# Lightning attention with balanced MoE on one core: two-input rank arithmetic, digits on VectorE, an earlier compaction operand, and ten weight loads queued ahead of the first gathers

## The chip, the cores and the metric

The kernel runs on one core of a Trainium2 chip. The metric is the device time of one execution in microseconds (us). Each kernel of a comparison ran on the same chip as the kernel before, in alternating rounds. A run is called slow if it is over 1.5% above the fastest run of the same kernel. Two terms of the profile: the DMA share is the mean busy share of the core's 16 DMA engines (the sum of the packets' times, which can come out over 1: 1.15 from 131 to 155 us in the kernel before), and the granted clock is TensorE's clock as a share of full speed (0.895 on average there).

## The reference

Four sequences of 768 tokens, 8 heads of 64, go through a decaying linear attention. The result, 3072 tokens of 512, is routed to 8 experts with a capacity of 384 each, in the order of the largest logit anywhere, and each token goes through its expert's two matrices.

```python
def _moe_ref(x, w_gate, w1, w2):            # x: 3072 x 512, w1: 8 x 512 x 1024, w2: 8 x 1024 x 512
    logits = x @ w_gate
    flat = logits.flatten()
    order = np.argsort(-flat)
    # ... greedy: a token takes the expert of its pair if it has none and the expert has room (cap = N // E)
    for e in range(E):
        mask = assigned == e
        h = np.maximum(x[mask] @ w1[e], 0.0)
        out[mask] = h @ w2[e]
```

## The kernel before

It has three stages. **Attention** works through 24 tiles of 128 tokens with a hand-made order of instructions; each tile's q, k and v are loaded on SyncE's queue, and its result xs is stored to DRAM there. **Routing** ranks the logits by counting, and gives the token numbers (`perm`) of each expert. The **experts** gather their tokens with indirect DMAs, run two matmuls, and scatter the result. All weight loads (sixteen of 1 MB), gathers and scatters are issued by GpSimd, in program order. In this kernel's trace no recorded landing of that queue comes before that of an earlier issue: the load issued at 180.40 landed at 198.28, the scatter issued at 181.53 at 198.92, and the one issued at 183.82, behind one more load, at 204.59.

```python
# attention: 256 bytes of each token and head go to each place in SBUF
def _load(self, g, name, src):
    b, t = divmod(g, 6)
    a = self.io.tile([128, 8, 64], F32, tag=name, name=name)
    self.nc.sync.dma_start(out=a, in_=src[b, :, t * 128 : (t + 1) * 128, :].rearrange("h p d -> p h d"))
# ...
d["xs"] = self.wk.tile([128, 4, 2, 64], F32, tag="xs", name="xs", bufs=3)   # stored to x_dram

# ranks of a group of tiles: one-input operations on VectorE
y = rc.tile([P, n], F32, name=f"y{a}")
V.tensor_scalar(y, vc, self.lo[:, 0:1], self.sc[:, 0:1], OP.add, OP.mult)
V.tensor_scalar(y, y, 1.0, self.VB - 1.0, OP.max, OP.min)
# ...

# the experts' order of issue; later holds the weight loads that are left
later = list(later)                          # range(8, 16)
for _ in range(2):                           # right after the gathers of experts 0 and 1
    moe.load_w(later.pop(0))
# ... two more when the next token numbers come
def experts():
    for n in range(16):
        # ...
        yield from moe.up(jobs[n], n % 8)
        # ... transposes of the next expert, gathers of the expert after the next three
        if later:
            moe.load_w(later.pop(0))
        for c in range(len(jobs[n]["perms"])):
            yield from moe.down(jobs[n], n % 8, c)      # matmuls, copy to oe (4 buffers), scatter
            if later and c == 0:
                moe.load_w(later.pop(0))
```

Of the kernel before, what the change touches and what calls it, by code (L numbers as in the profile page):

```python
# [23 lines left out]
class _Router:  # L24
# [11 lines left out]
    def constants(self):  # L36
# [36 lines left out]
        V.memset(self.ind2[:, 64:128, :], 0.0)  # L73
        self.i_kt = iota("i_kt", [P, P, 24], [[1, P], [0, 24]], 1)
# [17 lines left out]
        self.gbase = iota("gbase", [1, 9, 24], [[384, 9], [0, 24]], 1, 0, F32)  # L92
# [54 lines left out]
    def ranks(self, L, a, b):  # L147
# [7 lines left out]
        V.tensor_scalar(y, vc, self.lo[:, 0:1], self.sc[:, 0:1], OP.add, OP.mult)  # L155
        V.tensor_scalar(y, y, 1.0, self.VB - 1.0, OP.max, OP.min)
        V.tensor_scalar(zc, y, MAGIC, MAGIC, OP.add, OP.subtract)
# [8 lines left out]
        V.tensor_scalar(y, zc, 1.0 / 4096.0, -0.5 + 1.0 / 8192.0, OP.mult, OP.add)  # L166
        V.tensor_scalar(q1, y, MAGIC, MAGIC, OP.add, OP.subtract)
# [18 lines left out]
    def extras(self, L, a, b):  # L186

        nc, rc, P = self.nc, self.rc, 128
        V, G = nc.vector, nc.gpsimd
        n = b - a  # L190
        Z = rc.tile([P, n, 8], F32, name=f"Z{a}")
        H = rc.tile([P, n, 8], F32, name=f"H{a}")
        G.tensor_scalar(Z, L[:, a:b, :], self.lo[:, 1:2], self.sc[:, 1:2], OP.add, OP.mult)
        G.tensor_scalar(Z, Z, 1.0, self.ZB - 1.0, OP.max, OP.min)
        G.tensor_scalar(Z, Z, MAGIC, MAGIC, OP.add, OP.subtract)
        G.tensor_scalar(H, Z, 1.0 / 1024.0, -0.5 + 1.0 / 2048.0, OP.mult, OP.add)
        G.tensor_scalar(H, H, MAGIC, MAGIC, OP.add, OP.subtract)
        G.tensor_copy(self.zp[:, a:b, :, 0], H)
        G.tensor_scalar(H, H, -1024.0, None, OP.mult)
        G.tensor_tensor(self.zp[:, a:b, :, 1], Z, H, OP.add)  # L200

    def warm(self, us):

        for _ in range(int(us / 0.11) if self.spare is not None else 0):
            self.nc.tensor.matmul(self.spare, self.identb,
                                  self.i_kt.rearrange("p k t -> p (k t)")[:, 0:256],
                                  start=True, stop=True)
# [12 lines left out]
    def first(self, L, sp):  # L220
# [32 lines left out]
        for t in range(22, 24):  # L253
# [7 lines left out]
        _, nm2 = settle(count(z2, lambda: self.more(1)), self.ones[64])  # L261
        z3 = sp.tile([P, 24], BF16, name="z3")
        V.tensor_scalar(z3, zB, nm2, 100.0, OP.subtract, OP.min)
        nps, nm3 = settle(count(z3), self.ones[1])
        self.extras(L, 0, 24)
# [6 lines left out]
        V.tensor_tensor(Gm, self.i_g8, g8[:, None, :].to_broadcast([P, 9, 24]), OP.is_equal)  # L272
        cum = sp.tile([P, 9, 24], BF16, name="cum")
# [3 lines left out]
        pos = ps.tile([P, 9, 24], F32, tag="pos")  # L277
        posf = pos.rearrange("p g t -> p (g t)")
        nc.tensor.matmul(posf, self.ones3[0:1, :], self.gbase.rearrange("p g t -> p (g t)"),
                         start=True, stop=False)  # L280
        nc.tensor.matmul(posf, self.sltm, Gm.rearrange("p g t -> p (g t)"), start=False,
                         stop=False)
        nc.tensor.matmul(posf, self.ones[1], cum.rearrange("p g t -> p (g t)"), start=False,
                         stop=True)
        cps9 = ps.tile([P, 9], F32, tag="cnt")
        nc.tensor.matmul(cps9, self.ones[1], cum[:, :, 23], start=True, stop=True)
        sl = sp.tile([P, 9, 24], F32, name="sl")
        V.tensor_tensor(sl, pos, Gm, OP.mult)
        slot = sp.tile([P, 24], F32, name="slot")
        V.reduce_sum(slot, sl.rearrange("p g t -> p t g"), axis=AX.X)  # L290
# [18 lines left out]
        self.warm(3.0)  # L309
        for t in range(24):  # L310
            nc.tensor.matmul(pe1, A[:, :, t], B1v[:, :, :, t], start=(t == 0), stop=(t == 23))
        perm0 = st.tile([P, 6], I32, name="perm0")
        with nc.allow_low_precision(reason="token numbers are exact"):
            V.reduce_sum(perm0, pe1.rearrange("p a j -> p j a"), axis=AX.X)
        yield perm0.rearrange("p (e j) -> p e j", j=3)

# [6 lines left out]
                        zpv[:, :, None, :].to_broadcast([P, 24, 5, 16]), OP.mult)  # L323
        V.tensor_tensor(R5[:, :, :, 16], B5, self.i_t[:, 0:5, :].rearrange("p j t -> p t j"),
# [3 lines left out]
        self.warm(1.2)  # L328
# [61 lines left out]
    def steps(self, rest):  # L390
# [24 lines left out]
        for i in range(1, 7):  # L415
# [6 lines left out]
            for r in range(3):  # L422
                ind = sp.tile([P, 5, P], BF16, tag="indc")
                for c in range(5):
                    V.tensor_scalar(ind[:, c, :], self.kvec[r], zr[:, c : c + 1], None, OP.is_le)  # L425
# [74 lines left out]
        for c in range(5):  # L500
            V.tensor_scalar(A5[:, c, :], self.kvec[2], slot[:, c : c + 1], None, OP.is_equal)
# [251 lines left out]
def _exact_path(ctx, tc, L, router, moe, dram):  # L753
# [150 lines left out]
    nc.tensor.matmul(ppf, router.ones3[0:1, :], router.gbase[:, 0:8].rearrange("p g t -> p (g t)"),  # L904
# [19 lines left out]
class _Attn:  # L924
# [11 lines left out]
    LATE = dict(kph=(82.8, 86.36, 90.63, 92.36, 102.76, 107.19, 110.24), kpl=(84, 87.49,  # L936
                93.13, 94.38, 105.5, 109.86, 113.46), vs=(86.47, 89.87, 92.11, 99.11,
                100.13, 107.97, 116.19, 117.82), vh=(87.64, 94.24, 95.44, 100.66, 101.71,
                111.46, 118.28, 118.97), vl=(88.74, 96.24, 97.98, 101.76, 103.5, 112.33,
                119.71, 122.06), Tq=(82.96, 86.42, 92.65, 96.65, 100.91, 105.29, 108.01,  # L940
                113.13), qh=(84.83, 87.13, 93.73, 97.36, 102.25, 106, 109.73, 113.84),
                ql=(85.66, 88.14, 95.79, 98.86, 104.12, 107.25, 111.66, 114.86), Tk=(85.37,
                87.02, 89.58, 95.81, 102.12, 107.15, 112.29, 115.02), kT=(86.26, 88.74,
                91.35, 97.65, 103.44, 108.53, 113.6, 119.27), S=(87.48, 91.55, 97.86,
                102.58, 106.43, 110.74, 115.48, 120.03), h0=(83.51, 88.45, 94.78, 99.49,
                103.55, 108.56, 113.17, 116.45, 121), h1=(84.17, 89.11, 93.07, 98.83,
                104.21, 107.9, 112, 117.11, 122.17), l0=(84.34, 89.34, 96.39, 101.57,
                104.72, 109.79, 114.2, 117.35, 125.19), l1=(85, 90.61, 93.92, 100.31,
                105.38, 109.13, 112.94, 118.01, 125.93), m0=(85.25, 90.89, 97.37, 102.89,
                107.36, 111.72, 117.21, 120.84, 126.01), m1=(85.86, 91.5, 95.63, 101.15,  # L950
                106.75, 111.11, 115.58, 121.45, 126.75), I=(88.2, 92.27, 96.27, 100.53,
                104.28, 108.93, 112.75, 117.51, 122.23, 126.09), X=(88.83, 93.11, 97.11,
                101.37, 104.54, 109.99, 113.59, 118.14, 123.05, 127.49), ST=(84.69, 90.41,
                0, 99.85, 105.75, 109.31, 114.34, 121.21, 0), sth=(85.85, 91.34, 0, 101.2,
                106.68, 110.95, 115.27, 122.83, 0), stl=(83.7, 87.54, 92.72, 0, 102.23,
                107.85, 112.34, 116.67, 123.98, 0), xs=(90, 94.58, 98.25, 102.83, 106.64,
                111.05, 116.06, 119.87, 124.58, 129.11), Tx=(84.23, 91.09, 95.35, 99.02,
                103.67, 108.47, 111.83, 116.83, 120.75, 125.35, 129.88), xh=(85.34, 91.85,
                96.06, 100.15, 104.87, 109.22, 112.66, 117.77, 121.66, 126.29, 130.82),
                xl=(86.86, 93.32, 97.05, 100.97, 106.04, 110.45, 115.46, 118.67, 123.38,  # L960
                128.51, 131.5), G=(83.86, 90.04, 94.11, 99.48, 103.3, 107.61, 111.46,
                116.22, 119.43, 124.43, 129.27, 132.26), lg=(87.46, 91.27, 95.71, 100.23,
                104.04, 108.45, 112.26, 117.27, 120.48, 125.85, 130.08, 133.07))
# [290 lines left out]
def kernel(  # L1254
# [22 lines left out]
    moe = _Moe(ctx, tc, identb, x_dram, moe_w1, moe_w2, out, 8)  # L1277
    with ExitStack() as actx:
        attn = _Attn(actx, tc, q, k, v, lam, moe_w_gate, identf, logits, x_dram)
        const_steps = router.constants()  # L1280
        steps, end = router.constants(), attn.END
        others = [(t, lambda: next(steps, None))
                  for t in (-3.0, -1.0, 3.5, end + 123.19, end + 129.5)]
        others += [(end + t, lambda i=i, h=h: router.ranges(logits, 14, h and attn.spare(h), i))
                   for i, (t, h) in enumerate(((91.95, 0), (94.48, 15), (95.19, 0),
                                               (98.58, 16), (99.46, 0)))]
        others += [(end + t, lambda a=a, b=b: router.ranks(logits, a, b))
                   for t, a, b in ((120.57, 0, 16), (126.60, 16, 22))]
        others += [(end + t, lambda m=m: moe.load_w(m)) for m, t in
                   enumerate((104.63, 108.99, 114.71, 118.84, 126.0, 126.1, 126.2, 126.3))]  # L1290
        with tc.manual_schedule():
            attn.run(others)
    moe.open(ctx)
    fi = _route_and_moe(ctx, tc, logits, router, moe, range(8, 16))
    _check_and_mend(ctx, tc, logits, router, moe, dram, fi)


# [28 lines left out]
```

## Time and profile before

| | us |
|---|---|
| median of 4 runs (range) | 292.0 (291.58 to 293.32) |
| profiled span | 290.0 |
| last logits | 140.39 |
| first token numbers (perm) | 156.95 |
| first transposes of gathered tokens | 164.55 |
| oe copies held by scatters | 16.6, in three waits |

The prediction below shows the stretches, waits and timelines of this kernel. The first lines are from the timeline of SyncE's queue, with start, length, queue and operation in the columns:

```profile
97.93 0.37 SPq L1017 DMA_DIRECT2D qf<-in_q_dram  x1
99.62 0.34 SPq L1193 DMA_DIRECT2D x_dram<-xs  x1
100.70 0.37 SPq L1017 DMA_DIRECT2D vf<-in_v_dram  x1
```

GpSimd's first weight load of this kernel, in its timeline, with start, length, queue and operation in the columns:

```profile
106.25 1.01 POOL L576 DMA_DIRECT2D w<-in_moe_w_dram  x1
```

### The profile page before, as it was taken

How to read it: one execution, taken by the hardware profiler on the slowest of the kernel's cores; microseconds unless marked ns; L12 is line 12 of the kernel's file. 1: busy time of each engine (PE TensorE's matmuls, PEld its weight loads, DVE VectorE, ACT ScalarE, POOL GpSimd, SP SyncE). 2: the span in 40 equal slices, each digit the busy share in tenths (PEclk: the TensorE clock that was granted, in tenths of full speed). 3: DMA queues.
4: the chain of work that ended last, by engine and by line, in shares of the span. 5: the costliest groups of instructions: out<-in, count | busy, mean ns of one | idle time of the engine just before them, and what ended most of it. 6: DMA issues, size and time to landing. Idle time of an engine off the chain costs nothing.

```text
span 290.0 us, 8784 instructions
## 1 busy us (share of the span) xinstructions
PE 231.8 (80%) x3552; PEld 184.0 (63%) x3552; DVE 185.2 (64%) x570; ACT 154.9 (53%) x273; POOL 188.5 (65%) x212
## 2 busy tenths in 40 slices
PE   1779999999999899845562799990698999899970
PEld 0669888988888688734442676660455776577740
DVE  5688989898989999998658768780276750000000
ACT  6588888888897678520000144520325654576640
POOL 8999999999999889955522866542533155454220
PEclk9999999999999999995555579996589999999995
DMA  6999999989899839999993699999995236334121
GB/s 148 253 229 245 251 268 244 250 217 239 218 221 217 221 82 199 229 232 227 222 209 64 72 182 204 209 209 238 231 240 159 75 91 128 94 95 84 63 77 43
DMA packets 96977, 52.06 MB, mean 179 GB/s; under 512 B 76960, under 2 KB 88224, under 8 KB 96928
## 3 DMA queue, kind: packets, MB, share of 16 engines
q0 software_dynamic: 17920, 26.22, 46.9%
q1 hardware_dynamic: 79008, 25.19, 35.3%
q8 instruction: 30, 0.49, 0.7%
q14 instruction: 19, 0.16, 0.2%
HBM read 58.74 MB, written 12.58 MB: 246 GB/s over the span
## 4 chain that ended last, share of the span: by engine, by line
PE 44%; DMA 18%; DVE 12%; POOL 10%; issue 10%; ACT 4%; POOLq 0%; ACTq 0%; DVEq 0%
DMA out_dram<-oe,perm 12%; PE p L638 7%; PE p L625 6%; DMA w<-in_moe_w_dram 5%; PE XL L1155 4%; PE S L1097 4%; PE kT_ps L1079 4%; PE stp L1168 4%; PE xT_ps L1200 4%; POOL kp L1037 3%; PE qT_ps L1060 3%; PE XL L1144 2%; POOL vl L1054 2%; PE XL L1223 2%; POOL xe L594 2%
## 5 line engine op out<-in xcount | busy, mean ns | idle before, releaser
L625 PE MATMUL p<-xeT,w 128*128 128x256 bf16 (+1 forms) x512 | 52.0, 255 | 12.8 <-ACT hT L630 11.2
L625 PEld LDWEIGHTS <-w 128*128 128x128 bf16 x512 | 39.9, 100 | 21.2 <-issue 15.1
L644 POOL DMA_INDIRECT out_dram<-oe,perm x24 | 24.2, 1008 | 42.2 <-ACT oe L643 32.5
L594 POOL DMA_INDIRECT xe<-x_dram,perm x24 | 26.5, 1104 | 33.4 <-DVE B L319 11.1
L638 PE MATMUL p<-w,hT 128*128 128x512 bf16 x192 | 45.7, 383 | 0.0
L630 ACT ACTIVATE hT<-p 128x512 bf16<-128x512 f32 (+1 forms) x64 | 31.2, 491 | 18.8 <-PE p L625 13.9
L1103 ACT CAST sp<-S 128x512 bf16<-128x512 f32 x48 | 32.9, 748 | 12.7 <-PE S L1097 12.7
L643 ACT COPY oe<-p 128x512 f32<-128x512 f32 x24 | 14.1, 586 | 41.1 <-PE p L638 24.5
L1113 DVE TENSOR_TENSOR sp<-S,sp 128x512 bf16<-128x512 f32 x48 | 33.4, 741 | 3.8 <-ACT sp L1103 3.5
L1124 POOL TENSOR_SCALAR_AFFINE_SELECT sp<-sp 128x512 f32<-128x512 f32 x48 | 30.1, 638 | 8.4 <-DVE sp L1113 4.3
L1037 POOL TENSOR_TENSOR kp<-kf,kp 128x512 f16<-128x512 f32 x24 | 30.8, 1288 | 0.4 <-ACT kp L1033 0.4
L638 PEld LDWEIGHTS <-hT 128*128 128x128 bf16 x192 | 17.2, 98 | 17.2 <-issue 0.5
L1054 POOL TENSOR_TENSOR vl<-vs,vh 128x512 bf16<-128x512 f32 x24 | 27.9, 1165 | 0.1
L612 ACT COPY xeT<-pt 128x1024 bf16<-128x1024 bf16 (+1 forms) x16 | 12.8, 798 | 27.1 <-DVE ind L425 26.6
L1043 POOL TENSOR_TENSOR vs<-vf,lamneg 128x512 f32<-128x512 f32 x24 | 25.1, 1048 | 0.0
L1155 PE MATMUL XL<-vh,sp 128*128 128x64 bf16 x384 | 21.5, 195 | 3.3 <-POOL sp L1124 2.7
L1097 PE MATMUL S<-qh,kT 64*128 64x128 f16 x384 | 21.8, 221 | 1.0 <-DVE kT L1085 1.0
L1206 ACT CAST xh<-xT_ps 128x512 bf16<-128x512 f32 x24 | 14.2, 592 | 15.5 <-PE xT_ps L1200 15.0
L1155 PEld LDWEIGHTS <-sp 128*128 128x128 bf16 x576 | 19.8, 99 | 3.8 <-POOL sp L1124 2.9
L1060 PE MATMUL qT_ps<-identf,qf 128*128 128x128 f32 x96 | 16.6, 298 | 6.1 <-DMA qf<-in_q_dram 5.6
L1097 PEld LDWEIGHTS <-kT 64*128 64x128 f16 x576 | 17.0, 96 | 6.0 <-issue 3.4
L1188 DVE TENSOR_TENSOR xs<-XL,lampow 128x512 f32<-128x512 f32 x24 | 16.5, 688 | 6.3 <-PE XL L1155 6.0
(255 smaller groups left out, 559.0 us busy)
## 6 DMA issues: line engine op xcount, KB each, us to landing
w<-in_moe_w_dram POOLq DMA_DIRECT2D x16, 1024.0 KB, 15.2
kf<-in_k_dram SPq DMA_DIRECT2D x24, 256.0 KB, 4.2
qf<-in_q_dram SPq DMA_DIRECT2D x24, 256.0 KB, 4.2
vf<-in_v_dram SPq DMA_DIRECT2D x24, 256.0 KB, 4.5
x_dram<-xs SPq DMA_DIRECT2D x24, 256.0 KB, 4.1
xe<-x_dram,perm POOLq DMA_INDIRECT x24, 6.8
out_dram<-oe,perm POOLq DMA_INDIRECT x24, 3.3
lam_sb<-in_lam_dram SPq DMA_DIRECT2D x1, 4.0 KB, 2.9
```

What stands on the lines that cost most here:

```text
L594: nc.gpsimd.indirect_dma_start(out=xe[:, c, :], out_offset=None, in_=self.x_dram, in_offset=bass.IndirectOffsetOnAxis(ap=pm, axis=0), boun ...
L625: nc.tensor.matmul(p1[:, f, 0:n, :], self.w1t[e][:, kc, fc * P : (fc + 1) * P], j["xeT"][:, kc, 0:n, :], start=(kc == 0), stop=(kc == 3), ...
L630: nc.scalar.activation(hT[:, fp, :, 0:n, :], p1[:, :, 0:n, :], ACT.Relu)
L638: nc.tensor.matmul(p2, j["hT"][:, kc // 2, kc % 2, c, :], self.w2t[e][:, kc, :], start=(kc == 0), stop=(kc == 7))
L1037: self.nc.gpsimd.tensor_tensor(d["kp"][:, :, :, 0], d["kf"], d["kp"][:, :, :, 1], OP.subtract)
L1054: self.nc.gpsimd.tensor_tensor(d["vl"], d["vs"], d["vh"], OP.subtract)
L1060: self.nc.tensor.transpose(d["qT"][:, hp, :], d["qf"][:, 2 * hp : 2 * hp + 2, :].rearrange("p h d -> p (h d)"), self.identf)
L1097: self.nc.tensor.matmul(d["S"][a][:, hp, :], d["kT"][r, hp, :, ks], qq[r, hp, :], start=(i == 0), stop=(i == 2))
L1103: self.nc.scalar.copy(d["sp"][a][:, :, :, 1], d["S"][a])
L1113: self.nc.vector.tensor_tensor(s[:, :, :, 0], self.d[g]["S"][a], s[:, :, :, 1], OP.subtract)
L1124: self.nc.gpsimd.affine_select(out=sf, in_=sf, compare_op=OP.is_ge, fill=0.0, base=0, pattern=[[0, 4], [1, 128]], channel_multiplier=-1)
L1155: self.nc.tensor.matmul(d["XL"][:, a, hp, :], d["sp"][a][:, hp, :, ss], vv[:, h, :], start=(first and hp == 0 and i == 0), stop=(i == 2), ...
```

## The change

Its intent: VectorE's small rank operations should no longer wait for GpSimd; GpSimd should have less to do ahead of the gathers; two more weight loads (the whole of five experts instead of four) should be moved before the gathers, and the first of them begun earlier. The order of attention's instructions was made anew to fit. (The rank operations scale each token's largest logit to a whole number; the digits are the high and the low part of every logit scaled so; the compaction collects the tokens that have no place yet, with B5 and R5 as its operands. The masks below are GpSimd's operations on sp in attention.)

```diff
+        cst = rc.tile([P, 3, 24], F32, name="cst")
+        for i, c in enumerate((MAGIC, self.VB - 1.0, -0.5 + 1.0 / 8192.0)):
+            V.memset(cst[:, i, :], c)
# ... rank arithmetic
-        V.tensor_scalar(y, vc, self.lo[:, 0:1], self.sc[:, 0:1], OP.add, OP.mult)
-        V.tensor_scalar(y, y, 1.0, self.VB - 1.0, OP.max, OP.min)
+        V.scalar_tensor_tensor(y, vc, self.lo[:, 0:1], self.sc[:, 0:1].to_broadcast([P, n]),
+                               OP.add, OP.mult)
+        V.scalar_tensor_tensor(y, y, 1.0, top, OP.max, OP.min)
# ... digits: eight G. operations become seven V. operations, in the waits for two counts
# ... positions: [P, 9, 24] becomes [P, 24, 9], so that the reduction is contiguous
# ... compaction: B5 and R5 move ahead of perm0 and the first gathers
# ... five tensor_scalar comparisons become one tensor_tensor; warm() goes
-    moe = _Moe(ctx, tc, identb, x_dram, moe_w1, moe_w2, out, 8)
+    moe = _Moe(ctx, tc, identb, x_dram, moe_w1, moe_w2, out, 10)
-                   enumerate((104.63, 108.99, 114.71, 118.84, 126.0, 126.1, 126.2, 126.3))]
+                   enumerate((97.16, 102.15, 106.71, 112, 116.44, 127.0, 127.1, 127.2, 127.3, 127.4))]
-    fi = _route_and_moe(ctx, tc, logits, router, moe, range(8, 16))
+    fi = _route_and_moe(ctx, tc, logits, router, moe, range(10, 16))
# ... the tables of attention's order (not shown)
```

## The prediction

> **What bounds the kernel now.** I read the page, then the chain of waits, then cut the span into stretches at the places where the DMA share changes. In this view each row is a stretch in us, then its length, busy us of the engines, granted TensorE clock, DMA share and GB/s.
>
> ```profile
> 98.00:107.00 9.00, 8.17 (x198) 7.49 (x195) 8.89 (x21) 6.87 (x12) 7.86 (x9) 1.00 0.49 142
> 107.00:131.00 24.00, 18.76 (x439) 16.66 (x437) 23.29 (x43) 14.10 (x25) 20.33 (x27) 0.98 1.08 206
> 131.00:155.00 24.00, 12.28 (x158) 9.67 (x157) 16.92 (x53) 1.17 (x2) 9.41 (x13) 0.50 1.15 213
> 155.00:161.00 6.00, 2.33 (x30) 2.21 (x30) 4.76 (x8) 0.00 (x0) 2.75 (x2) 0.50 0.03 4
> 161.00:166.00 5.00, 4.59 (x54) 4.32 (x51) 3.48 (x18) 0.26 (x1) 4.38 (x5) 0.50 0.74 86
> 166.00:196.00 30.00, 29.25 (x259) 20.31 (x260) 23.12 (x139) 13.01 (x20) 16.30 (x17) 0.92 1.16 199
> 196.00:206.00 10.00, 0.36 (x4) 0.12 (x3) 0.36 (x3) 1.89 (x4) 2.98 (x3) 0.61 1.19 233
> ...
> 250.00:290.00 40.00, 30.65 (x343) 21.87 (x340) 0.00 (x0) 19.85 (x47) 12.41 (x13) 0.92 0.28 76
> ```
>
> DMA is full (share over 1.0) from 107 to 155, empty for 155 to 161, and full again to about 221. TensorE does nothing from 196 to 206, while DMA is at its fullest. Who makes it wait is in the table of waits (us in total, times, longest):
>
> ```profile
> ACT oe L643 <- DMA out_dram<-oe,perm: 16.6, 3, 7.8
> ```
>
> and in the timeline of ScalarE, where the two long idle times stand in brackets:
>
> ```profile
> 199.02 0.59 ACT L643 COPY oe<-p 128x512 f32<-128x512 f32 x1 [7.80 <-DMA out_dram<-oe,perm]
> 204.69 0.59 ACT L643 COPY oe<-p 128x512 f32<-128x512 f32 x1 [5.09 <-DMA out_dram<-oe,perm]
> ...
> 217.34 0.59 ACT L643 COPY oe<-p 128x512 f32<-128x512 f32 x1 [3.67 <-DMA out_dram<-oe,perm]
> ```
>
> There are four oe buffers; the fifth and sixth copy need scatters one and two to have landed. Those were issued at 181.53 and 183.82 and landed only at 199.0 and 204.6, because GpSimd's queue is served in order and five, then six, late weight loads stand before them. So between 165 (first late load) and 205 the end is set by DMA work, not by routing; after 205.8, by TensorE work (84.2 us to the end, with one more 1.56 us gap at 216.9 for scatter four).
>
> Before that, the routing sets when the first tokens are gathered. The VectorE and GpSimd timelines show two places where it loses time:
>
> ```profile
> 99.63 2.04 POOL L1043 TENSOR_TENSOR vs<-vf,lamneg 128x512 f32<-128x512 f32 x2
> 100.73 0.96 DVE L140 SCALAR_TENSOR_TENSOR lo<-rg,mb 128x2 f32<-128x2 f32 x1
> ...
> 123.02 2.92 DVE L155 TENSOR_SCALAR y<-r_v,lo,sc 128x16 f32<-128x16 f32 x1
> ...
> 131.60 2.55 POOL L576 DMA_DIRECT2D w<-in_moe_w_dram  x3
> 134.13 0.67 POOL L1124 TENSOR_SCALAR_AFFINE_SELECT sp<-sp 128x512 f32<-128x512 f32 x1
> ...
> 157.49 2.16 DVE L322 TENSOR_TENSOR R<-B,r_zp 128x1920 f16<-128x1920 f16 x1
> 157.96 2.73 POOL L594 DMA_INDIRECT xe<-x_dram,perm  x1 [11.10 <-DVE B L319]
> ```
>
> A 16-element operation takes 2.92 us instead of some 0.2, while GpSimd is busy without a gap; a mask (134.13) stands behind three weight issues though its input was ready at 131.56; and a gather issue takes 2.73 us instead of 1.0 beside a long multiplication.
>
> [...] the 2.92 us operation waits through two masks, a subtraction and two iotas. [...] the two-input form at 100.73 took 0.96 us, ending with the second GpSimd multiplication (101.67). [...]
>
> **The change part by part.**
> *Rank arithmetic.* For tiles 0 to 15 the five small operations cost 2.92+0.26+0.17+0.29+0.17 = 3.8 us. In the new form some 0.2 each, but the first can still wait for masks and the subtraction (until 124.9 in the old order): I take 1.0 plus 1.3 of waiting, a gain of 1.5. For tiles 16 to 21, 0.29+0.47+0.75+0.17+0.65 = 2.3 us become 1.0, partly beside TensorE. The loads move behind the last mask: 2.5 us of its wait go. Attention should end some 3 us sooner (137.5, was 140.5). Five loads (0.85 us each) plus the moved iotas (1.9) now run on GpSimd before slt is ready; this ends near 137 and can eat a few tenths.
> *Digits.* Eight GpSimd operations go[...]. Their seven VectorE forms (0.2 to 0.25 each, 1.5 in all) lie where VectorE waits for TensorE counts (gaps of 0.74 and 1.46 us): free.
> *Transposed positions.* The reduction of 216 strided elements takes 0.63, contiguous about 0.4; but the product and two matmuls now read with a stride. Net 0 to 0.2.
> *Compaction operand ahead of the gathers.* B5 and R5, 0.3 and 2.16, start when the last indicator ends (155.85 in the old time) and TensorE is done at 156.9: perm0 comes about 1.5 us later. In return both first gathers issue in 1.0 us[...]. Second gather about 0.4 to 0.8 us sooner.
> *Five single-column comparisons become one.* 0.90 us become about 0.83 (640 elements[...], from 120-element and 1920-element rows). Off the path.
> *warm* issues nothing: its spare is None, so its removal is worth 0.
> The sum so far: gathers can issue about 4 us sooner, near 155 instead of 158 to 160.
> *Ten loads.* A load moves 1.05 MB at the 200 to 213 GB/s of the full stretches: 5.2 us. Two more before the gathers are 10.5 us. They start about 98.5 instead of 106.6; the DMA share of 0.49 in that stretch leaves room for about 4.5 us of work. So the early queue empties at 154.7 + 10.5 − 4.5 = 160.7. **The gathers, ready at 155 to 160, then stand behind weights until about 160.7**; the four of them are 2.6 us, and the first late load starts near 163, where it was 165.2. Scatters one and two still have five and six late loads before them, in program order, so the stall's end moves only by the same 2.2 us, 205.8 to 203.6. After it, the last two loads no longer delay scatters three and four: the 1.56 us gap goes. Total 2.2 + 1.6 = 3.8 us: 292.34 − 3.8 = **288.5**.
>
> **The rivals.**
> 1. *Routing is what counts:* all 4 us arrive, and the stall shrinks besides. Then 283 to 286. For it: the chain runs through routing from 140 to 164. Against: the DMA queue's work before scatter two is now all sixteen loads instead of fourteen, so an earlier gather buys nothing while weights are moving.
> 2. *Two loads less in the late phase take their full 10.5 us away:* about 282. For it: DMA-full from 166 to 221. Against: the loads that leave stand behind scatter two, not before it.
> 3. *The gathers' new wait is longer:* if the early loads begin later than 98.5 or share badly with attention's loads, the queue empties at 163 or later; the start of experts does not move, only the 1.6 us stay: 290.5 to 292.
> 4. *VectorE still waits:* GpSimd's arithmetic blocks two-input forms too; attention gains 1 us instead of 3. Hidden behind the queue anyway: 288.5 to 289.5.
>
> **Range and chances.** The main error is when the early queue empties (±1.5 us) and whether the stall's length follows (±1.5). That gives 285.4 to 291.2. Faster by 2% needs 286.5, which asks for 2 us more than I count, from rival 1 or 2: 0.24. Slower by 2% needs a new stall: 0.02.
>
> **What would show it.** Operation y of 16 elements falls from 2.92 to under 1.7; the last mask directly follows the last sp; DMA share over 1.0 without a hole from 107 to over 200; first transposes of xe at 162.5 to 164, although perm0 is ready before 155.5; the idle time of the oe copies still shows two waits of several us ending near 202.5, and no third. I am wrong if the oe wait is gone or far shorter (then the order of the scatters mattered less than I think), or if the gathers land before 160.

## The result

| | before | after |
|---|---|---|
| median of 4 runs (range), us | 292.0 (291.58 to 293.32) | 303.38 (301.06 to 304.24) |

The ratio is 1.037, 95% interval 1.030 to 1.044: slower. (A ratio here is the mean time of one kernel's fast runs over that of the other's fast runs in the same rounds, so it is not quite the ratio of the medians.) The prediction was wrong in the sign and outside its range.

The same view of stretches as in the prediction, for the changed kernel (stretch, length, busy us of PE, PEld, DVE, ACT and POOL, granted clock, DMA share, GB/s):

```profile
98.00:107.00 9.00, 5.57 (x92) 4.97 (x93) 8.58 (x15) 2.58 (x5) 6.71 (x8) 0.85 1.04 202
107.00:131.00 24.00, 17.35 (x306) 15.43 (x303) 12.76 (x23) 11.71 (x20) 13.14 (x16) 0.78 1.10 226
131.00:155.00 24.00, 15.52 (x325) 13.39 (x322) 19.46 (x50) 7.05 (x13) 14.20 (x19) 0.71 0.71 131
155.00:161.00 6.00, 3.78 (x49) 3.53 (x50) 5.15 (x18) 0.00 (x0) 0.00 (x0) 0.50 1.14 212
```

Attention falls apart from 98 on. VectorE was busy 23.29 of 24 us in 107 to 131; now it is busy 12.76. The DMA engines are full from 98, where they had a share of 0.49. The hole at 155 to 161 is filled, as predicted, but a new one has opened in 131 to 155 (share 0.71; 0.12 from 139 to 147).

The table of waits names two that fit, each with us in total, times and the longest:

```profile
ACT oe L642 <- DMA out_dram<-oe,perm: 12.1, 2, 7.0
DVE xs L1187 <- DMA x_dram<-xs: 8.1, 2, 4.8
```

The xs operation now waits for its own stores, which it did not before. The timeline of SyncE's queue in the changed kernel, after 99:

```profile
99.33 7.67 SPq L1192 DMA_DIRECT2D x_dram<-xs  x1
107.10 0.71 SPq L1016 DMA_DIRECT2D vf<-in_v_dram  x1
107.90 4.11 SPq L1016 DMA_DIRECT2D kf<-in_k_dram  x1
112.11 3.26 SPq L1016 DMA_DIRECT2D qf<-in_q_dram  x1
```

And its first three weight loads in GpSimd's timeline:

```profile
97.51 0.98 POOL L575 DMA_DIRECT2D w<-in_moe_w_dram  x1
102.55 0.96 POOL L575 DMA_DIRECT2D w<-in_moe_w_dram  x1
111.71 0.79 POOL L575 DMA_DIRECT2D w<-in_moe_w_dram  x1
```

The first weight load is issued at 97.51, in the middle of attention's loads. Issues on SyncE's queue that took 0.34 to 0.37 us at this point before now take 0.7 to 7.7. The end of attention and the first numbers stand in VectorE's timeline:

```profile
99.15 3.50 DVE L142 TENSOR_SCALAR rg<-mb 128x2 f32<-128x2 f32 x1
...
137.12 1.18 DVE L160 SCALAR_TENSOR_TENSOR y<-r_v,lo,sc 128x16 f32<-128x16 f32 x1
...
152.39 0.16 DVE L1231 COPY logits<-Lo 128x8 f32<-128x8 f32 x1
...
169.92 0.16 DVE L321 TENSOR_REDUCE perm<-pe 128x6 int32<-128x12 f32 x1
```

So the last logits come 12.0 us later than before (152.39 for 140.39) and perm 13.0 us later. In ScalarE's timeline the second held oe copy starts at 216.42, 11.7 us later than before, and the third wait is gone. With 11.7 lost and the gap of 1.56 us saved, some 10 us are accounted for; the two profiled spans differ by 9.2.

**Below the page.** The trace holds each DMA packet with its queue, size and time. Their clock starts before the span does: the span's first instruction is at 10.4 us of it in the kernel before and at 10.5 in the changed one (the hole at 166.3 to 171.7 of it is 155.9 to 161.3 of the span). Two things were found.

First, the 73,728 packets of 256 bytes, which are attention's q, k and v, took 18.0 ns each on average before and 20.5 ns after; 0.5% were over 22 ns before, 22% after. In the compiled programs the tiles that they fill start at a multiple of 512 bytes in a partition before, and at 288 past one after: the little `cst` tile of 288 bytes moved everything allocated later. The times agree in direction with the shift; why a packet into a shifted tile takes longer isn't shown. The xs tile is shifted too: the 2048-byte packets of its stores went from 94 ns on average to 99 in the changed kernel and 107 in e2 below. The operations on these tiles show no such cost: GpSimd's kp subtraction takes 1288 ns before and 1281 after, VectorE's xl 682 and 681.

Second, attention's packets slow down when weight packets move beside them. These are packets that started per us, counted from the changed kernel's records over 2 us each, without packets of 4 bytes:

```
packet clock   256 B (q,k,v)   weight packets, mean size
106 to 108         694              0
112 to 114          83             82   2048 B
114 to 116          88             90   2048 B
116 to 118         717             46   1420 B
118 to 120          51            188   1024 B
126 to 128         115             92   2048 B
```

As soon as weight packets move, attention's packets go from some 700 per us to some 90, about one for each weight packet of 2048 bytes (those take 173 ns in the median); where the weight packets are few (116 to 118) they are back at some 700. The ratio isn't fixed, though (41 to 93 at 128 to 130, 51 to 188 at 118 to 120), and the records do not show what decides it: the fall in rate is what is measured. A load of 256 KB is 1024 packets, 1.5 us at 700 per us and 11 us at 90: an estimate from these counts. In the changed kernel, 5141 packets of attention's loads start after the first weight packet; in the kernel before none do.

The theory, called B in the expectations: the loss comes from weight loads begun while attention's own loads are still in the queue, beside which the small packets starve; the shifted tiles make attention's loads later, so more of them are caught.

### The profile page after: what moved, and what is told of

It is laid out like the page before. It is cut to its first block, busy times and chain, and to the rows that moved or that the text cites. A ratio compares the mean times of both kernels' runs of the same rounds, so it can differ in the third digit from the quotient of the medians.

```text
span 299.2 us, 8737 instructions
## 1 busy us (share of the span) xinstructions
PE 235.6 (79%) x3552; PEld 187.3 (63%) x3552; DVE 183.8 (61%) x504; ACT 155.1 (52%) x273; POOL 183.2 (61%) x204
## 4 chain that ended last, share of the span: by engine, by line
PE 39%; DMA 21%; DVE 14%; POOL 10%; issue 10%; ACT 3%; SPq 0%; POOLq 0%; ACTq 0%; DVEq 0%
DMA x_dram<-xs 8%; PE p L637 8%; PE p L624 7%; DMA out_dram<-oe,perm 7%; DMA xe<-x_dram,perm 5%; PE stp L1167 3%; PE S L1096 3%; PE xT_ps L1199 3%; PE XL L1154 3%; PE kT_ps L1078 3%; POOL kp L1036 2%; POOL vl L1053 2%; DVE sp L1112 2%; PE XL L1143 2%; PE qT_ps L1059 2%
## 5 line engine op out<-in xcount | busy, mean ns | idle before, releaser
L624 PE MATMUL p<-xeT,w 128*128 128x256 bf16 (+1 forms) x512 | 51.0, 252 | 11.9 <-ACT hT L629 9.3
L643 POOL DMA_INDIRECT out_dram<-oe,perm x24 | 25.2, 1050 | 46.2 <-ACT oe L642 36.7
L593 POOL DMA_INDIRECT xe<-x_dram,perm x24 | 25.5, 1064 | 37.6 <-DVE perm L321 18.7
L637 PE MATMUL p<-w,hT 128*128 128x512 bf16 x192 | 45.0, 378 | 0.0
L1036 POOL TENSOR_TENSOR kp<-kf,kp 128x512 f16<-128x512 f32 x24 | 30.7, 1281 | 1.6 <-ACT kp L1032 1.5
L1059 PE MATMUL qT_ps<-identf,qf 128*128 128x128 f32 x96 | 17.5, 310 | 10.0 <-DMA qf<-in_q_dram 6.4
L1096 PE MATMUL S<-qh,kT 64*128 64x128 f16 x384 | 22.5, 226 | 1.7 <-DVE kT L1084 1.4
L1154 PE MATMUL XL<-vh,sp 128*128 128x64 bf16 x384 | 23.0, 201 | 0.0
L1096 PEld LDWEIGHTS <-kT 64*128 64x128 f16 x576 | 17.8, 99 | 6.7 <-issue 3.8
L1154 PEld LDWEIGHTS <-sp 128*128 128x128 bf16 x576 | 21.4, 103 | 0.3
```

The costliest lines, as they stand in the source:

```text
L593: nc.gpsimd.indirect_dma_start(out=xe[:, c, :], out_offset=None, in_=self.x_dram, in_offset=bass.IndirectOffsetOnAxis(ap=pm, axis=0), boun ...
L624: nc.tensor.matmul(p1[:, f, 0:n, :], self.w1t[e][:, kc, fc * P : (fc + 1) * P], j["xeT"][:, kc, 0:n, :], start=(kc == 0), stop=(kc == 3), ...
L637: nc.tensor.matmul(p2, j["hT"][:, kc // 2, kc % 2, c, :], self.w2t[e][:, kc, :], start=(kc == 0), stop=(kc == 7))
L643: sc = nc.gpsimd.indirect_dma_start(out=self.out, out_offset=bass.IndirectOffsetOnAxis(ap=j["perms"][c], axis=0), in_=oe, in_offset=None, ...
L1036: self.nc.gpsimd.tensor_tensor(d["kp"][:, :, :, 0], d["kf"], d["kp"][:, :, :, 1], OP.subtract)
L1096: self.nc.tensor.matmul(d["S"][a][:, hp, :], d["kT"][r, hp, :, ks], qq[r, hp, :], start=(i == 0), stop=(i == 2))
```

## The experiments

Eighteen kernels ran, all with correct results. Medians of before in the five groups of runs were 291.96 (e1 to e4), 292.48 (e5 to e8), 292.79 (e9 to e12), 292.08 (e13 to e16) and 292.03 (e17 and e18).

### Tiles and number of loads

**e1_pad**: the tiles are moved back to multiples of 512 bytes by a longer tile ahead of them.

```diff
-        n_idx = cp.tile([P, 6], F32, name="n_idx")
+        n_idx = cp.tile([P, 62], F32, name="n_idx")[:, 0:6]
```

> The kernel after, with 224 unused bytes behind n_idx and nothing else: the new constant tile of 288 bytes had moved attention's q, k, v and xs tiles from a multiple of 512 bytes to 32 bytes past a multiple of 256, and the padding moves them back. Theory P (placement: a 256-byte packet into such a tile costs more, attention's transfers fall behind): 286 to 291 us, packets of 256 bytes at a median of 18 ns all through, no wait of xs for the x_dram store. Theory W (the weight loads begin at 97 us, while attention's own transfers are still running, and starve the x_dram stores[...]): 299 to 304 us, with the waits of xs for x_dram still there. Theory B (it takes both): about 289 here, and each of the next two near 292.

**e2_shift**: the kernel before, with `cst` and its three memsets added and nothing else.

> The kernel before with the new constant tile of 288 bytes added (filled, not used), so that attention's tiles move by 288 bytes and nothing else changes but three small fills. P: slower, 295 to 302 us, and packets of 256 bytes well over 18 ns on average. W: 292 us, unchanged. B: 292 to 294, packets slower but hidden, as the loads begin only at 106 us.

**e3_l8**: the changed kernel with eight early loads, begun as before; the tiles stay shifted.

```diff
-    moe = _Moe(ctx, tc, identb, x_dram, moe_w1, moe_w2, out, 10)
+    moe = _Moe(ctx, tc, identb, x_dram, moe_w1, moe_w2, out, 8)
-                   enumerate((97.16, 102.15, 106.71, 112, 116.44, 127.0, 127.1, 127.2, 127.3, 127.4))]
+                   enumerate((104.63, 108.99, 114.71, 118.84, 127.0, 127.1, 127.2, 127.3))]
# ... and range(8, 16) for the loads that are left
```

> The kernel after with eight early loads at the times of the kernel before (the last four behind the last mask, as in the kernel after); tiles shifted. W: 288 to 292 us, no wait of xs for x_dram. P: still 297 to 303. B: 289 to 293.

**e4_pad_l8**: both edits.

> Both of the above: padded, and eight early loads. All theories: 287 to 291 us, which is what rank arithmetic, digits and compaction bring alone (about 4 us sooner gathers). If it is 299 or more, the cause is neither placement nor the loads but the new order of attention's instructions.

| | tiles | begin, early loads | us (fast runs' ratio to before) | 256-byte packet, ns | after first weight packet |
|---|---|---|---|---|---|
| after | shifted | early, 10 | 303.38 (1.037) | 20.5 | 5141 |
| e1 | aligned | early, 10 | 290.9 (0.996) | 18.1 | 1536 |
| e2, before + `cst` | shifted | as before, 8 | 292.48 (1.001) | 20.4 | 79 |
| e3 | shifted | as before, 8 | 290.0 (0.994) | 20.1 | 0 |
| e4 | aligned | as before, 8 | 290.77 (0.996) | 18.0 | 0 |

In these runs neither the shift nor the early begin is slow alone (e9, and perhaps e6, qualify this for the early begin below). The shift alone does make attention's loads later: by the packet records the last of them starts at 109.57 of the span in e2 (103.31 before) and at 105.52 in e3 (101.33 in e4). Note that e1 is no gain: its stall ends at 204.82, where the kernel before ends it at 204.69. In VectorE's timeline of e1:

```profile
98.77 3.50 DVE L142 TENSOR_SCALAR rg<-mb 128x2 f32<-128x2 f32 x1
...
141.41 0.16 DVE L1231 COPY logits<-Lo 128x8 f32<-128x8 f32 x1
```

And in that of e4:

```profile
98.61 0.80 DVE L142 TENSOR_SCALAR rg<-mb 128x2 f32<-128x2 f32 x1
99.45 0.54 DVE L144 SCALAR_TENSOR_TENSOR lo<-rg,mb 128x2 f32<-128x2 f32 x1
...
122.64 3.25 DVE L160 SCALAR_TENSOR_TENSOR y<-r_v,lo,sc 128x16 f32<-128x16 f32 x1
```

This is a third effect of the early begin. In the changed kernel the load's issue, 1 us long, moves four GpSimd operations in a row to 98.51; the one-input operation rg, begun at 99.15, takes 3.50 us, until the last of the four is done, and TensorE stands 3.35 us behind it. In e5, where the same four start at 97.49, rg takes 0.80 us and ends with the second. All eight profiles of the changed order with the early begin show 3.49 to 3.51 us there, and the eight with the later begin some 0.8 for rg and 0.54 for the next operation, lo. It looks like the wait of the operation at 123.02 in the prediction (2.92 us, ending with GpSimd's second iota), come back at another place. It doesn't make the loss by itself, and the loss doesn't need it: e1 has it and is not slow, and e13 below is slow without it. But it isn't free: e1's last logits come 3.2 us later than e4's, although no wait for attention's transfers is longer, while TensorE's longest wait for VectorE's ql goes from 1.0 to 3.4 us. How much of the changed kernel's 12.0 us it carries was not separated.

### Time of begin, and the order of scatters and loads

**e5_late10**: ten loads with shifted tiles, but the first five begun later.

```diff
-                   enumerate((97.16, 102.15, 106.71, 112, 116.44, 127.0, 127.1, 127.2, 127.3, 127.4))]
+                   enumerate((104.63, 108.99, 112.0, 116.44, 118.84, 127.0, 127.1, 127.2, 127.3, 127.4))]
```

> The changed kernel, tiles still shifted by 288 bytes, still ten weight loads before the gathers, but the first five of them issued at the places in attention's schedule where the kernel before issued its first four (nominal 104.63 to 118.84) and the other five at the end of attention. Theory B (the time goes when weight loads begin while attention's own 256-byte packets, slowed by the shifted tiles, still wait in the queue): under 300 packets of 256 bytes after the first weight packet, no wait of the xs operation for its store over 1 us, last logits at 138 to 141, total 289.5 to 292. Rival N (ten loads before the gathers are too many, whenever they begin): last logits at 145 or later and a total over 296.

Measured: 290.66 us (289.08 to 294.36, the last slow), ratio 0.997; no 256-byte packet after the first weight packet; last logits at 138.90. For attention's delay it is not the number of loads that counts, but their begin.

**e6_pad_defer**: e1, with two loads moved behind scatter four. **e7_before_defer**: the same edit on the kernel before, where it moves four loads.

```diff
-                if later:
+                if later and n >= 2:
                     moe.load_w(later.pop(0))
                 for c in range(len(jobs[n]["perms"])):
                     yield from moe.down(jobs[n], n % 8, c)
-                    if later and c == 0:
+                    if later and n >= 2 and c == 0:
```

> The changed kernel with the tiles moved back to multiples of 512 bytes (290.9 us in an earlier run), and with the two weight loads that stand before scatters one and two in program order moved behind scatter four. The prediction's first step (the stall of the oe copies is set by the weight loads that stand before scatters one and two in GpSimd's queue): the waits of oe for the scatters, 6.1 and 5.1 us, shrink by about 5 us for the first and 10 us for both, to under 2 us in sum, and the total falls to 281 to 286. Rival (DMA bandwidth over the whole late phase is the limit, so the wait only moves to later weights or scatters): the sum of waits of ScalarE and TensorE in the late phase stays above 9 us, total 288.5 to 291.

> The kernel before with the one edit of e6: of its eight late loads, the four that are issued with the first two experts (two of them before scatters one and two) wait until the third and fourth. If the order of scatters and loads sets the stall: the waits of oe, 7.8, 5.1 and 3.7 us, shrink to under 5 us in sum, total 281 to 286. If bandwidth sets it: 290 to 293, with a wait for weights in TensorE later on.

Measured: e6 281.44 us (three runs 279.93 to 281.68, one slow of 288.74), ratio 0.958; e7 284.68 us, ratio 0.972. The waits for scatters in e7 are 10.3 us in sum (16.6 before), not under 5 as expected. Those of e1, and then of e6, in the tables of waits:

```profile
ACT oe L642 <- DMA out_dram<-oe,perm: 11.2, 2, 6.1
```

```profile
ACT oe L642 <- DMA out_dram<-oe,perm: 1.3, 1, 1.3
```

So the order of scatters and loads carried the stall, as the prediction's first step had it, and the rival of mere bandwidth falls. Four deferred loads bring back part of the wait, two nearly none.

**e8_off64**: the tiles at 64 bytes past a multiple of 512 (a longer `n_idx` again). **e9_off256**: at 256 past one.

> The changed kernel, with its ten early loads, and with the attention tiles 64 bytes past a multiple of 512 rather than 32 bytes past a multiple of 256. If what counts is that the tiles start at a multiple of 64 bytes, packets of 256 bytes take 18.0 to 18.3 ns and the total is 290 to 292; if every start that is not a multiple of 256 costs, they take 20 to 21 ns and the total is 299 to 305.

> The changed kernel with ten early loads, the attention tiles at 256 past a multiple of 512 bytes. If a start at a multiple of 256 is enough for a 256-byte packet: packets of 256 bytes take 18.0 to 18.3 ns, total 290 to 292 as with the tiles at multiples of 512. If a multiple of 512 is what they need: 20 to 21 ns and 299 to 305.

Measured: e8's packets took 20.5 ns, e9's 18.2. So of the four starts tried (0, 64, 256 and 288 past a multiple of 512) the two multiples of 256 are quick (18.0 to 18.2 ns, against 20.5). In time neither is clean. e8 had three executions of 301.59 to 306.11 and one of 292.41; the three are slow against the one, so the comparison is open. e9 had four of 289.21 to 291.33 and one of 301.23, the profiled one, in which xs waits 5.7 us for its store and 3325 packets come after the first weight packet. An early begin can thus end on either of two courses, and the aligned tiles don't rule out the bad one.

### Two by two, and again

**e10_early8**: e3's kernel with its first four loads begun early (97.16, 102.15, 106.71, 112). **e11_again**: the changed kernel unchanged. **e12_late10_defer**: aligned tiles, e5's ten times, e6's order.

> The changed kernel, tiles shifted by 288 bytes, with eight weight loads before the gathers instead of ten, but the first four begun as early as the change begins them (nominal 97.16 to 112). It completes a table of two by two with e3 (eight, later: 290.0) and e5 (ten, later: 290.7). Theory B (the early begin counts, with the shift): last logits at 147 to 153, over 2500 packets of 256 bytes after the first weight packet, total 298 to 304. Rival (early begin and ten loads are both needed): last logits before 143, total 290 to 293.

> The changed kernel as it is, once more, in five rounds, because the run with the tiles at 64 bytes had one execution of 292.4 among three of 301.6 to 306.1. If the slow course is a matter of chance from execution to execution: one or two of the six at 290 to 293. If the shift with the early loads always leads to it: all six at 299 to 306.

> A candidate: the changed kernel with the tiles moved back, all ten early loads begun as in e5 (nominal 104.63), and the two loads before scatters one and two moved behind scatter four as in e6 (281.4). If the remaining contention of early loads with attention costs what the logits show (141.4 to 141.7 rather than 138.2 to 138.5): the logits come at 138 to 139, total 278 to 281. If the gathers stand behind the weights anyway: 281 to 282.5.

| shifted tiles | 8 early loads | 10 early loads |
|---|---|---|
| begun later | 290.0 (e3) | 290.66 (e5) |
| begun early | 306.92 (e10) | 303.38; e11 303.79 |

e10 is slower than expected (298 to 304), while its last logits, at 152.22, and its 4498 packets after the first weight packet are as expected. e11's six executions lie between 298.46 and 308.0 (ratio of the fast three 1.027), none near 290. Over all kernels with shifted tiles and early begin (after, e8, e10, e11, e13, e14) 24 of 26 executions are at 297 us or more (11 of them slow, so this is a count and no comparison of times). With aligned starts and early begin (e1, e6, e9) one of 13 shows the bad course in its profile, and e6's 288.74 may be a second; it has no trace. Of those begun later, without deferral (e2 to e5), none of 16 is at 297 or more. That is how far "shift and early begin" is settled: the early begin is needed, the shift makes the bad course almost certain.

e12 measured 280.11 us (279.59 to 281.01), ratio 0.957.

### What else could take part

**e13_before_early**: the kernel before with only `cst` added and its first four loads begun at 97.16, 102.15, 106.71 and 112.

> The kernel before with two things alone: the 288-byte constant tile that shifts attention's tiles, and its first four weight loads begun as early as the change begins them (nominal 97.16 to 112). Theory B (these two suffice): last logits at 147 or later, over 2500 packets of 256 bytes after the first weight packet, total 298 to 307. Rival (the new order of attention's instructions is part of it): total 290 to 294.

Measured: 301.65 us (297.48 to 306.31; two fast runs of 297.48 and 298.86, two slow), with before at 290.98 to 293.74; both fast runs lie above every run of before. In the profile, of the 297.48, 3544 packets come after the first weight packet and the last logits at 146.45 (expected 147 or later). These stand in its table of waits:

```profile
DVE xs L1192 <- DMA x_dram<-xs: 5.9, 2, 5.1
POOL vs L1047 <- DMA vf<-in_v_dram: 3.3, 1, 3.3
```

With nothing else of the change in it a loss of 5.4 to 6.8 us is there in fast runs, and its rg and lo operations (0.96 us at most) have no long wait. TensorE's granted clock, lower in the changed kernel (0.85 in 98 to 107), is 1.00 there, so a lower clock isn't what starts it. Nothing else of the change is needed for a loss; whether the rest, rg's wait above all, makes up the difference to the changed kernel's 11 is open.

**e14_xs4**: the changed kernel with a fourth xs buffer.

```diff
-        d["xs"] = self.wk.tile([128, 4, 2, 64], F32, tag="xs", name="xs", bufs=3)
+        d["xs"] = self.wk.tile([128, 4, 2, 64], F32, tag="xs", name="xs", bufs=4)
```

> The changed kernel with four buffers for xs instead of three (it stands behind nearly all other attention tiles, which keep their odd starts). If the wait of xs for its store (8.1 us in the profile of the changed kernel) carries the loss: that wait goes and the total falls to 291 to 296. If it is only a sign, and attention's loads, slowed by weight packets, carry it: total 299 to 306, the idle time moves to operations that read q, k and v.

Measured: 302.5 to 313.12 us in three executions, one of 294.9. The three are slow against the one, so the time is not compared; the profile, of one of the three, shows no wait of xs for a store, and instead this line in the table of waits:

```profile
PE qT_ps L1059 <- DMA qf<-in_q_dram: 23.5, 2, 17.0
```

The shorter of the two, 6.6 us, is the first load at the kernel's start, which the kernel before waits for too (5.6); the 17.0 is new. In this run the wait for stores is a sign, and late q loads carry the loss.

**e15_l8_defer**: e4 with e6's order. **e16_l8_defer_old**: the same, with perm0 and the gathers ahead of B5 and R5, as in the kernel before.

> The changed kernel with tiles moved back, eight early loads begun as before, and no weight load between the first experts' scatters one to four (e4 was 290.8 with the old order of scatters and loads; e12, with ten loads, 280.1 with its first transposes at 166.4, behind weights). If the start of the experts counts once the stall is gone: first transposes at 161, total 274 to 278. If weights for later experts then come late: a wait for w in TensorE, total 279 to 283.

> As e15, but the token numbers are summed and the gathers issued ahead of the compaction operand, as the kernel before does it. If the prediction's price holds (token numbers 1.5 us later, in return the first gather issue 1.7 us faster): the first gather issues about 1.5 us earlier and takes 2.7 us instead of 1.0 to 1.25, the first transposes come within 0.5 us of e15, and the total is within 1 us of e15. If the order matters: a difference of 1.5 us or more.

Measured: 283.79 and 283.06 us (both with intervals that overlap widely, 0.968 to 0.977 and 0.959 to 0.974 of before). The first gather of e15 in GpSimd's timeline:

```profile
156.69 1.26 POOL L593 DMA_INDIRECT xe<-x_dram,perm  x1 [19.06 <-DVE perm L321]
```

And that of e16:

```profile
155.48 2.60 POOL L593 DMA_INDIRECT xe<-x_dram,perm  x1 [17.81 <-DVE B L319]
```

The operand ahead delays perm by 1.21 us (155.70 in e15, 154.49 in e16; predicted 1.5) and shortens the first gather issue from 2.60 to 1.26 us. The second gather's issue ends 0.35 us sooner (159.28 and 159.63; predicted 0.4 to 0.8), the first transposes 0.7 (162.33 and 163.04), which is not to be seen in the time. The miss of e15 is that it is slower than e12 (280.11, in another group) although its first transposes end 5.3 us sooner. Its four deferred loads bring back 10.1 us of oe waits; that they are the reason is argued, not shown.

**e17_l9_defer**: e12 with nine early loads, the first five begun as in e12. **e18_l9_one**: besides, each of the three deferred loads stands behind the first scatter of another expert. The diff is e18's against e17:

```diff
-                if later and n >= 2:
-                    moe.load_w(later.pop(0))
                 for c in range(len(jobs[n]["perms"])):
                     yield from moe.down(jobs[n], n % 8, c)
                     if later and n >= 2 and c == 0:
                         moe.load_w(later.pop(0))
```

> As e12 with nine early loads instead of ten, so seven late ones: four before scatters one and two as in e12, three deferred to the third and fourth expert. If the early queue then empties as the gathers are ready: first transposes near 162, at most a single oe wait of some 2 to 3 us, total 276 to 279. If the third deferred load brings back waits for scatters as in e15: total 280 to 283.

> As e17, but the three deferred loads are spread, one behind the first scatter of the third, fourth and fifth expert each. If a load costs the scatters time only where two of them stand together: no oe wait over 1 us, total 275 to 278. If weights come too late for the last experts instead: a wait for w in TensorE, total over 279.

Measured: e17 277.52 to 278.14 us in three executions, ratio 0.951, so within its first range, but with 10.2 us of oe waits in three, where one of 2 to 3 was expected. A fourth execution took 711.79 us. No trace of it exists, and what happened is open; the kernel ends with a check that can start a long repair, but whether it did was not recorded. e18: 276.51 us (276.13 to 276.83), ratio 0.947, interval 0.943 to 0.951. Its oe copies no longer wait for any scatter. That all of 10.2 us of waits went and the time fell by 1.6 shows that a wait of ScalarE is not a loss of time as long; what TensorE does counts. In the view of stretches, e15 from 196 to 226:

```profile
196.00:226.00 30.00, 25.07 (x214) 16.73 (x215) 18.65 (x92) 11.74 (x20) 16.20 (x15) 0.92 1.04 218
```

And e18:

```profile
196.00:226.00 30.00, 29.27 (x261) 19.50 (x262) 19.63 (x94) 15.88 (x25) 16.46 (x17) 1.00 1.00 199
```

TensorE goes from 25.07 to 29.27 busy us of 30 (27.38 in e17), and its granted clock from 0.92 to 1.00. e18 is the fastest of all, but with four executions and a near relation that once took 712 us, it should run many more times before it is used.

## Why the prediction was wrong

- **What bounds the late phase: right.** Scatters one and two behind weight loads set the stall. Changing that order alone takes away 7.8 us (e7 against before, same rounds) and some 9.5 (e6 against e1, in different groups).
- **Ten loads: the step that failed.** It reads "the DMA share of 0.49 in that stretch leaves room for about 4.5 us of work". The share was a mean over 98 to 107, and it was taken as room anywhere in that stretch. In the kernel before the last 256-byte packet starts at 113.7 of the packets' clock, 103.3 of the span's: the share is 0.68 up to there and 0.20 from there to 107. The loads begun at 97.5 met the fuller part, and beside them attention's packets fell from some 700 to some 90 per us. In place of 4.5 us gained the attention lost 12.0 (13.0 up to perm). Rival 3 had "share badly with attention's loads", but let it delay only the weights, never attention.
- **Where attention isn't starved, the 4.5 us are missing too.** The first transposes start at 166.29 in e1 (loads begun at 97.13) and at 166.59 and 166.35 in e5 and e12 (begun at 105.73 and 105.45), not at 162.5 to 164; it was 164.55 before. In e5's timeline of TensorE:

```profile
166.59 1.28 PE L607 MATMUL pt<-identb,xe 128*128 128x128 bf16 x8 [4.95 <-DMA xe<-x_dram,perm]
```

So ten loads hold the gathered tokens back until some 166, not 160.7, and beginning them over 8 us earlier brought 0.3 at most. In e1 the DMA share is 0.39 from 133 to 136: five loads were moved into attention, but the other five are issued behind its end (134.77). What is left is the outcome of rival 3, 290.5 to 292 (e1 290.9, e5 290.66).
- **What was missing altogether:** the 288 bytes of `cst`. The working doesn't mention it, nor where later tiles start. Packets of 256 bytes went from 18.0 to 20.5 ns; alone that costs nothing (e2, ratio 1.001), while with the early begin nearly every execution (24 of 26) takes the bad course.
- **Late loads from 163 and a stall end at 203.6: half right.** In e5, where attention is undisturbed, the first late loads are issued at 162.57 instead of 164.76, as predicted (its 165.2 for before stands in no view), but the held oe copy that ends the stall starts at 204.50, against 204.69 before and a predicted 202.5; the prediction's 203.6 is when TensorE goes on. From the first late load to that copy it is 41.9 us there and 39.9 before; the step "the stall's end moves only by the same 2.2 us" fails. The distance grows where the gathered tokens come late: TensorE waits for them, and the next gathers are issued at 171.04 instead of 168.75. No run tests this apart. In e1 the late loads start no sooner (165.13), and so the stall ends no sooner.
- **The third gap goes: right** in after, e1 and e5; it is back with eight loads (e3 and e4, 4.1 to 4.5 us). e1 and e5, 1 to 2 us below before, have nothing else to show for themselves at the stall, which ends where it did. e3 gains its 2 us the other way: the stall ends at 201.79, and the third wait stays.
- **Rank arithmetic: the size was off.** Where the loads begin later, logits come at 138.1 to 138.9 in seven of eight profiles, so 1.5 to 2.3 us sooner, not 3; in e17 they come 2.95 us sooner (137.44). The loads do stand behind the last mask. But the first y operation still takes 3.25 us in e4, until the last of a row of four GpSimd operations is done, 3.14 in e12 and 1.50 in e3, beside GpSimd arithmetic (0.92 in e17; the 1.18 of the changed kernel, under the 1.7 that was to show the gain, came with attention late anyway); the prediction's own finding, a two-input operation that took 0.96 us until a GpSimd multiplication ended, applied to the very operation it counted as 1.0 plus 1.3. Beside weight issues the new form lost nothing: in e4 four operations of 128 by 6 took 0.17 us each (132.17 to 132.94, within four issues), where the old one-input forms took 0.47, 0.75, 0.17 and 0.65 beside three. That the two-input form would wait less was the estimate in the prediction, with no run behind it then.
- **Digits and positions: 0.3 us rather than 1.0 to 1.2.** From the last logits to perm it was 16.56 us before and is 16.27 in e16, which has the old order of gathers. sl went from 0.38 to 0.52 us, the reduction from 0.63 to 0.38, which cancels as predicted. The digits' 1.0 us was the estimate of what VectorE loses beside the eight GpSimd operations. Before, the first rank operation after the last logits took 0.40 us, the pair of indicators 0.52, r_q and z 0.37 each; in the changed kernel it is 0.22, 0.42, 0.18 and 0.24. Where the rest went is not resolved.
- **Operand ahead of the gathers: right in kind, somewhat smaller in size** (e15 and e16). **The comparison of 640 elements: right**, 0.82 us. **warm: no separate test.**
- **The chance of slower, 0.02,** rested on "a new stall", without a place for one. The working looked for waits where operations were moved, not where transfers of another stage lay.

## What to carry to other kernels

Before a large transfer is begun earlier, look at when the last small transfer of the stage beside it starts, packet by packet if need be, rather than at the mean DMA share of the stretch. When a tile is added ahead of others, look at where the tiles filled by small DMA packets now start; a pad of 224 bytes settled the packets' times here (18.1 ns in e1, 20.5 without it), and the bad course in most executions; the later begin settled the course in all 16 that were counted. And where buffers wait for scatters, first change the order in which scatters and loads are issued: one condition gave 8 to 10 us, where the whole change, with its harm mended, gave 1 to 3. Last, when loads are moved ahead of gathers, count when the queue empties: nine loads (e17, e18) left the first transposes at 160.7 to 160.9, ten at some 166.
